# Values, row-tiled sinks and the next scores in one TensorE block, and sink v spread over partitions by DMA

## The chip, the cores and the metric

The kernel runs on one core of a Trainium2 chip. Its time is the device time of one execution in microseconds, and the median of a few executions is given. The core has five engines that work side by side: TensorE (PE) multiplies matrices, VectorE (DVE) and ScalarE (ACT) do elementwise work, GpSimd (POOL) does some too and issues DMAs that change the type, and SyncE (SP) issues DMAs only. Sixteen DMA engines move the data of all queues. TensorE writes to PSUM, which has eight banks of 128 partitions x 512 floats.

## The reference

Attention with a sliding window of 128 positions and 4 sink positions, and then a block of layer norm and MLP, over 4 batches, 8 heads, 768 positions, head size 64:

```python
scores = (1 / sqrt(D)) * q @ k.T                       # per batch and head
keep = (pos_k < 4) | ((pos_q - pos_k >= 0) & (pos_q - pos_k < 128))
a = softmax(where(keep, scores, -1e9))
x = (a @ v), heads side by side                        # (4, 768, 512)
xn = (x - mean(x)) / sqrt(var(x) + 1e-6) * g_ln
out = x + relu(xn @ w_ch1) @ w_ch2                     # w_ch1: 512 x 2048, w_ch2: 2048 x 512
```

## The kernel before

The 768 positions of a batch are 6 tiles of 128, so there are 24 tiles, t = 6 * batch + r. A plan orders all operations: each has a cost, a key (priority) and what it depends on, and the plan lays them out for each engine in the order in which they are then written into the program. The plan's dependencies decide the order only. What an instruction really waits for in the program comes from the buffers that it reads and writes.

The eight PSUM banks are two `wide` buffers of two banks (pool "pw") and four `single` buffers of one (pool "pm").

Scores of a tile: keys of 128 positions against queries of 256, for 8 heads. Two heads stand in the two halves of the 128 partitions, so each matmul has 64 rows:

```python
    def scores(t, halves, key):
        # ... pbs: one wide buffer for each half of the heads; ebs: where exp goes
        def mm(_):
            for pb, eb, part in zip(pbs, ebs, parts):
                # ... (tiles 0 to 2 first add a mask by matmul)
                for i, hp in enumerate([2 * half + i for half in part for i in range(2)]):
                    for h2 in range(2):
                        nc.tensor.matmul(pb.t[:, h2, i],
                                         lhsT=kb.t[64 * h2:64 * (h2 + 1), 1, hp, 128 * r:128 * (r + 1)],
                                         rhs=kb.t[64 * h2:64 * (h2 + 1), 0, hp, 128 * r:128 * r + n],
                                         start=not added, stop=True, skip_group_check=True)
        # ... then ACT takes the exp of each, and DVE or POOL masks it
```

Values of a tile: for each half of the heads (4 heads, 65 columns each: 64 of v and a one, for the sum of the weights), a sink part where r >= 2, the tile's own keys and those of the tile before:

```python
    def values(t, key):
        # ...
        pb = Buf("pw", 0)
        def mm(_):
            # ...
            for half in range(2):
                fresh = True
                if r >= 2:
                    nc.tensor.matmul(po[:, half, 0:4 * (D + 1)], lhsT=esb[b].t[:, 128 * (r - 2):128 * (r - 1)],
                                     rhs=vs[:, 4 * half:4 * half + 4, :].rearrange("p h d -> p (h d)"),
                                     start=True, stop=False, skip_group_check=True)
                    fresh = False
                for hh in range(4):
                    # ... matmul with vn[:, r, h, 0:D + 1], and if r > 0 with vn[:, r - 1, h, 0:D + 1]
        # then on DVE: rc = reciprocal of the sums, xt = values * rc, statistics, xn
```

`esb` holds exp of the sink scores: 8 rows (4 sinks of 2 heads) in each 32 of the 128 partitions. `vs` has the sinks' v at the same rows, each head's in its own rows and zero elsewhere. It is made by a matmul with a 0/1 matrix `sel`, which spreads the 4 sinks' rows of v over the partitions, and a DVE multiply with a mask:

```python
    def sinks(b, key):
        # ...
        def mm_v(_):
            # ...
            for half in range(2):
                nc.tensor.matmul(halves[half][:, 0:4 * (D + 1)], lhsT=sel,
                                 rhs=vn_buf[b % 2][:, 0, 4 * half:4 * half + 4, 0:D + 1],
                                 start=True, stop=True, skip_group_check=True)
        def mul_v(_):
            # ... vs = that * smask, one DVE instruction for each half
        # mm: sink scores, four matmuls of 512 columns into one single bank; ex: their exp
```

In what order a tile's parts come, and the up part of the MLP (the down part is alike):

```python
    def attention(t, key):
        scores(t, (0, 1), key)
        if t % RB:
            values(t - 1, key - 0.5)
        if t % RB == RB - 1:
            values(t, key + 1.0)

    def up(g, h0, key):
        # ... pb = Buf("pm", 0): one single bank
        #     4 matmuls of n columns for each block of 128 hidden units, then relu by ACT or DVE
```

At the start, q and k of the first batch come in pieces over several queues, are cast and transposed by TensorE, while `spin` matmuls of constants keep TensorE busy.

Of the kernel before, what the change touches and what calls it, by code (L numbers as in the profile page):

```python
# [8 lines left out]
FP32 = mybir.dt.float32  # L9
# [22 lines left out]
class Plan:  # L32
# [18 lines left out]
    def op(self, engs, fn, deps=(), key=0.0, alloc=(), uses=(), lat=0.0):  # L51
        o = Op(engs, fn, deps, key, alloc, uses)
        o.lat = lat
        self.ops.append(o)
        return o
# [108 lines left out]
def kernel(  # L164
# [28 lines left out]


    GROUPS = [2, 2, 2, 4, 4, 4, 4, 2]
    NB0 = 3
    NG = len(GROUPS)
    FIRST = [sum(GROUPS[:g]) for g in range(NG)]
# [33 lines left out]
    def room_for(buf):  # L232
        return wide[buf.slot // 2] if buf.pool == "pw" else single[buf.slot - 4]
# [88 lines left out]
    op({"POOL": 0.5}, const_sel, [begun], -499.4)  # L322
    sinks_done = op({"POOL": 0.9}, const_sinks, [begun], -440)

# [89 lines left out]
    def load_w(which, c, key, took=2.6):  # L417
# [7 lines left out]

        w_in[(which, c)] = load(0.85, took, go, key)


    prepped, kqb, turns = {}, {}, {}

# [67 lines left out]
    def sinks(b, key):  # L498

        ks, vs = ks_buf[b % 2], vs_buf[b % 2]  # L500
        kb = kqb[b]
        pb, eb = Buf("pm", 0), Buf("es", 2)
        esb[b] = eb

        def mul_k(_):
            nc.vector.tensor_tensor(
                ks[:, :, 0:2 * NS].rearrange("p a (i s) -> p a i s", i=2),
                kb.t[:, 1, :, 0:NS].unsqueeze(2).to_broadcast([128, HP, 2, NS]),
                hmask.unsqueeze(1).unsqueeze(3).to_broadcast([128, HP, 2, NS]), op=ALU.mult)

        vb = [Buf("pw", 0)] if b else [Buf("pm", 0), Buf("pm", 0)]

        def mm_v(_):
            if b:
                halves = [room_for(vb[0])[:, i] for i in range(2)]
            else:
                halves = [room_for(i) for i in vb]
            vb[0].t = halves
            for half in range(2):
                nc.tensor.matmul(halves[half][:, 0:4 * (D + 1)], lhsT=sel,  # L520
                                 rhs=vn_buf[b % 2][:, 0, 4 * half:4 * half + 4, 0:D + 1],
                                 start=True, stop=True, skip_group_check=True)

        def mul_v(_):
            for half in range(2):
                nc.vector.tensor_tensor(
                    vs[:, 4 * half:4 * half + 4], vb[0].t[half][:, 0:4 * (D + 1)].rearrange("p (h d) -> p h d", d=D + 1),
                    smask[:, 4 * half:4 * half + 4].unsqueeze(2).to_broadcast([128, 4, D + 1]), op=ALU.mult)

        def mm(_):  # L530
            pb.t = room_for(pb)
            for hp in range(HP):
                nc.tensor.matmul(pb.t[32 * hp:32 * (hp + 1), :], lhsT=ks[:, hp, :], rhs=kb.t[:, 0, hp, 256:S],  # L533
                                 start=True, stop=True, skip_group_check=True)

        def ex(_):
            eb.t = espool.tile([128, S - 256], BF16, name="es")
            nc.scalar.activation(eb.t, pb.t, AF.Exp, scale=scale)

        o1 = op({"DVE": 0.2}, mul_k, ready(b, range(HP), 0, NS, 0, 0) + [sunk.get(b - 2), sinks_done, edone.get((RB * b, 0)) if b else None], key, (), [kb])  # L540
        ov = op({"PE": 0.22}, mm_v, [vcast[(b, 0)], sinks_done, ones_done] + ready(b, range(HP), 0, 0, 256, S), key, vb)
        vs_done[b] = op({"DVE": 0.8}, mul_v, [ov, vread.get((b - 2, RB - 1))], key, (), vb)
        o2 = op({"PE": 0.4}, mm, [o1] + ready(b, range(HP), 0, 0, 256, S), key, [pb], [kb])
        sunk[b] = op({"ACT": 0.6}, ex, [o2], key, [eb], [pb])

    ebuf = {}

    def scores(t, halves, key):

        b, r = divmod(t, RB)  # L550
        kb = kqb[b]
# [9 lines left out]
        added = t < NEG_TILES  # L561

        def mm(_):
            for pb, eb, part in zip(pbs, ebs, parts):
                eb.t = epool.tile([128, 2, 512 // n, n], BF16, name="e")
                pb.t = room_for(pb).rearrange("p a (i c) -> p a i c", c=n)
                if added:
                    neg = (neg1 if r else neg0)[:, 0:n].unsqueeze(1).to_broadcast([128, 2, n])
                    for h2 in range(2):
                        nc.tensor.matmul(pb.t[:, h2], lhsT=ident, rhs=neg,  # L570
# [7 lines that stand above are left out]

        cost = 0.2 + 0.23 * n / 256 * len(halves) + (0.43 * len(halves) if added else 0.0)
        hps = [2 * half + i for half in halves for i in range(2)]  # L580
        o0 = op({"PE": cost}, mm, ready(b, hps, 128 * r, 128 * (r + 1), 128 * r, 128 * r + n) + [neg_done, edone.get((t - 1, 1)) if last else None], key, pbs + ebs, [kb])

        for pb, eb, part in zip(pbs, ebs, parts):
            def ex(_, pb=pb, eb=eb):
# [32 lines left out]
    xb, xnb, xtb, mvb, rsb, turned = {}, {}, {}, {}, {}, {}  # L617
    aggr = {}

    def values(t, key):  # L620
        b, r = divmod(t, RB)
        g, ti = where[t]
        vn, vs = vn_buf[b % 2], vs_buf[b % 2]
        pb = Buf("pw", 0)
        xb[t] = Buf("x", 14)
        xnb[t] = Buf("xn", 6)

        def mm(_):
            po = pb.t = room_for(pb)
            pv = po[:, :, 0:4 * (D + 1)].rearrange("p a (h d) -> p a h d", d=D + 1)  # L630
            for half in range(2):
                fresh = True
                if r >= 2:
                    nc.tensor.matmul(po[:, half, 0:4 * (D + 1)], lhsT=esb[b].t[:, 128 * (r - 2):128 * (r - 1)],  # L634
                                     rhs=vs[:, 4 * half:4 * half + 4, :].rearrange("p h d -> p (h d)"),
                                     start=True, stop=False, skip_group_check=True)
                    fresh = False
                for hh in range(4):
                    i, h2 = divmod(hh, 2)
                    h = 4 * half + hh  # L640
                    nc.tensor.matmul(pv[:, half, hh, :], lhsT=weights_of(t, half, i, h2, 0), rhs=vn[:, r, h, 0:D + 1],  # L641
                                     start=fresh and hh == 0, stop=(r == 0), skip_group_check=True)
                    if r > 0:
                        nc.tensor.matmul(pv[:, half, hh, :], lhsT=weights_of(t - 1, half, i, h2, 128),  # L644
                                         rhs=vn[:, r - 1, h, 0:D + 1], start=False, stop=True, skip_group_check=True)

        deps = [edone[(t, half)] for half in range(2)] + [vcast[(b, r)], ones_done]
        uses = [ebuf[(t, half)] for half in range(2)]
# [5 lines left out]
        if r >= 2:  # L654
            deps += [sunk[b], vs_done[b]]
            uses += [esb[b]]
            cost += 0.22
        o = op({"PE": cost}, mm, deps, key, [pb], uses)
        vread[(b, r)] = o

        rc = {}

        def recip(_):
            pv = pb.t[:, :, 0:4 * (D + 1)].rearrange("p a (h d) -> p a h d", d=D + 1)
            rc[0] = small.tile([128, 2, 4], FP32, name="rc")
            nc.vector.reciprocal(rc[0], pv[:, :, :, D])
            xb[t].t = xpool.tile([128, H, D], BF16, name="xt")
            nc.vector.tensor_tensor(xb[t].t.rearrange("p (a h) d -> p a h d", a=2), pv[:, :, :, 0:D],  # L668
                                    rc[0].unsqueeze(3).to_broadcast([128, 2, 4, D]), op=ALU.mult)

# [11 lines left out]
            nc.vector.scalar_tensor_tensor(xnb[t].t, in0=xf, scalar=mvb[g][:, ti, 0:1], in1=gb,  # L682
                                           op0=ALU.subtract, op1=ALU.mult)

        o = op({"DVE": 0.92}, recip, [o], key, [xb[t]], [pb])
        o = op({"DVE": 0.9}, stat, [o], key, (), [xb[t]])
        aggr[t] = o
        o = op({"DVE": 0.75}, cen, [o, gb_done], key, [xnb[t]], [xb[t]])
# [120 lines left out]


    def attention(t, key):
        scores(t, (0, 1), key)
        if t % RB:
            values(t - 1, key - 0.5)
        if t % RB == RB - 1:
            values(t, key + 1.0)


# [22 lines left out]
    for x in range(2):  # L841
        load_runs(1, 0, x, 0, H, 3.85, -436 + x)
    load_w(2, 3, -434)
    for r in range(RB):
        load_v(1, r, -430 + r)

    for b in range(B):
# [25 lines left out]
        if b == 1:  # L873
            for hp in range(HP):
                prep_runs(1, 0, hp, k0 - 12 + 3 * hp)
        else:
            for r in range(RB):
                for x in range(2):
                    load_qk(b, x, r, k0 - 60 + r, [prepped.get((b - 1, RB - 1, 1))])
            for r in range(RB):  # L880
                load_v(b, r, k0 - 50 + r, [prepped[(b, RB - 1, 1)]])
        for r in range(RB):
            attention(RB * b + r, akey(RB * b + r))
            if r == 1:
# [55 lines left out]
```

The softmax here doesn't subtract the row's maximum and nothing guards it: scores larger than these inputs give would overflow.

## Time and profile before

| | |
|---|---|
| time, median of 3 runs | 225.98 us (225.73 to 226.04) |
| span of the profiled execution | 224.5 us |
| TensorE busy | 217.9 us (97%) |
| VectorE, ScalarE, GpSimd busy | 115.3, 111.8, 81.3 us |
| matmuls of the MLP (lines 745 and 785) in the chain that ended last | 34% and 37% |
| bytes moved by DMA | 25.59 MB, 84774 packets |

The profile is of one execution on the chip. A group's line has the source line, engine, operation, the buffers written and read, shapes, count, then busy time and mean duration of one in ns, and the idle time of the engine just before them. A timeline's line has start, duration, engine, source line, operation, buffers and count. Matmuls are pipelined, so their durations overlap: what one costs is read from the start of one to the start of the next.

### The profile page before, as it was taken

The page shows a single profiled execution, that of the slowest core. Times are in us where ns is not written, and L with a number is a line of the kernel's source. Part 1 is how long each engine was busy: PE and PEld are TensorE (multiplying, and loading weights), DVE is VectorE, ACT ScalarE, POOL GpSimd, SP SyncE. Part 2 cuts the span into 40 slices and gives each one's busy share as a digit, 9 for nine tenths or more (in the row PEclk, how much of TensorE's full clock was granted, in tenths as well). Part 3 has the DMA queues.
Part 4 walks back from the last instruction along what each step waited for, and adds up shares of the span by engine and source line. Part 5 has one row for each costly group of instructions (what it writes and reads, how often), then busy time and mean ns, then how long its engine had stood idle before and what let it go on. Part 6 is the DMA issues. An engine that isn't in the chain of part 4 may idle for free.

```text
span 224.5 us, 4431 instructions
## 1 busy us (share of the span) xinstructions
PE 217.9 (97%) x1805; PEld 123.4 (55%) x1826; DVE 115.3 (51%) x216; ACT 111.8 (50%) x159; POOL 81.3 (36%) x111
## 2 busy tenths in 40 slices
PE   8999999999999999999999999999999999999994
PEld 7565878884546455455454444544454554444852
DVE  5556876044978779589574467470026750021011
ACT  3689775677342585870327762147613157400620
POOL 8985976269420699350833000220006020000000
PEclk9999999999999999999999999999999999999999
DMA  6999999999999599999899011230002130012102
GB/s 166 154 190 198 191 206 204 204 160 155 133 137 260 131 151 149 147 131 180 90 170 233 12 23 48 87 103 0 0 36 85 47 96 0 0 47 93 50 0 93
DMA packets 84774, 25.59 MB, mean 114 GB/s; under 512 B 74385, under 2 KB 81809, under 8 KB 84754
## 3 DMA queue, kind: packets, MB, share of 16 engines
q0 software_dynamic: 59392, 13.24, 69.2%
q1 hardware_dynamic: 24818, 11.67, 25.4%
q10 hardware_dynamic: 544, 0.39, 0.5%
q8 instruction: 14, 0.23, 0.4%
q14 instruction: 6, 0.05, 0.1%
HBM read 27.27 MB, written 6.29 MB: 149 GB/s over the span
## 4 chain that ended last, share of the span: by engine, by line
PE 90%; DVE 7%; issue 1%; ACT 0%; DVEq 0%
PE single L785 37%; PE single L745 34%; PE wide L574 5%; PE single L236 3%; PE wide L641 2%; PE wide L644 2%; DVE xn L682 2%; DVE st L674 2%; DVE xt L668 2%; PE wide L634 1%; PE wide L457 1%; PE wide L570 1%; PE single L721 1%; PE single L457 1%; PE single L533 1%
## 5 line engine op out<-in xcount | busy, mean ns | idle before, releaser
L745 PE MATMUL single<-xnt,w1s 128*128 128x256 bf16 (+1 forms) x503 | 87.1, 325 | 0.6 <-issue 0.2
L745 PEld LDWEIGHTS <-w1s 128*128 128x128 bf16 x512 | 48.5, 98 | 32.6 <-issue 1.9
L585 ACT ACTIVATE e<-wide 128x1024 bf16<-128x1024 f32 x44 | 43.7, 1022 | 43.3 <-PE wide L574 40.8
L785 PE MATMUL single<-w2s,h1t 128*128 128x512 bf16 x249 | 57.6, 379 | 0.4
L798 DVE SCALAR_TENSOR_TENSOR ot<-single,rs,xt 128x512 f32<-128x512 f32 (+2 forms) x25 | 18.2, 729 | 60.2 <-PE single L785 45.1
L754 ACT ACTIVATE h1t<-single 128x512 bf16<-128x512 f32 x60 | 35.8, 597 | 20.9 <-PE single L745 20.9
L785 PEld LDWEIGHTS <-h1t 128*128 128x128 bf16 x256 | 24.0, 98 | 28.2 <-issue 1.1
L785 PE MATMUL single<-w2s,h1n 128*128 128x512 bf16 (+2 forms) x139 | 29.6, 355 | 0.3
L754 ACT ACTIVATE h1n<-single 128x512 bf16<-128x512 f32 x30 | 17.9, 597 | 22.2 <-PE single L745 22.0
L597 POOL TENSOR_SCALAR_AFFINE_SELECT e<-e 128x512 bf16<-128x512 bf16 (+1 forms) x10 | 7.1, 713 | 44.8 <-ACT e L585 44.8
L407 POOL DMA_DIRECT2D vn<-in_v_dram x24 | 21.6, 918 | 2.5 <-DMA qkn<-in_q_dram 1.1
L694 POOL TENSOR_SCALAR ve<-mv 128x2 f32<-128x2 f32 (+1 forms) x8 | 4.6, 574 | 45.8 <-DVE mv L677 45.6
L595 DVE TENSOR_TENSOR e<-e,mask 128x1024 bf16<-128x1024 bf16 x22 | 15.9, 722 | 8.7 <-ACT e L585 8.5
L785 PEld LDWEIGHTS <-h1n 128*128 128x128 bf16 x144 | 12.6, 98 | 12.3 <-issue 1.3
L682 DVE SCALAR_TENSOR_TENSOR xn<-xt,mv,gb 128x512 bf16<-128x512 bf16 x24 | 18.6, 780 | 0.8
L674 DVE BATCH_NORM_STATS2 st<-xt 128x6 f32<-128x512 bf16 x24 | 16.7, 695 | 0.8
L668 DVE TENSOR_TENSOR xt<-wide,rc 128x512 bf16<-128x512 f32 x24 | 16.6, 691 | 0.8
L641 PE MATMUL wide<-vn,e 128*128 128x65 bf16 x192 | 15.8, 193 | 0.0
L641 PEld LDWEIGHTS <-e 128*128 128x128 bf16 x192 | 13.7, 97 | 2.6 <-issue 0.2
L574 PE MATMUL wide<-qkt 64*128 64x256 bf16 (+1 forms) x192 | 14.5, 263 | 0.0
L644 PE MATMUL wide<-vn,e 128*128 128x65 bf16 x160 | 14.2, 193 | 0.0
L398 POOL DMA_DIRECT2D qkn<-in_q_dram x12 | 11.3, 940 | 3.5 <-DMA qkn<-in_k_dram 3.0
(66 smaller groups left out, 162.5 us busy)
## 6 DMA issues: line engine op xcount, KB each, us to landing
out_dram<-ot SPq DMA_DIRECT2D x23, 256.0 KB, 2.2
vn<-in_v_dram POOLq DMA_DIRECT2D x24, 128.0 KB, 8.0
w1s<-in_moe_w_ch_dram POOLq DMA_DIRECT2D x4, 512.0 KB, 11.9
w2s<-in_moe_w_ch_dram POOLq DMA_DIRECT2D x4, 512.0 KB, 14.5
qkn<-in_q_dram POOLq DMA_DIRECT2D x12, 128.0 KB, 7.6
qkn<-in_k_dram POOLq DMA_DIRECT2D x12, 128.0 KB, 7.0
qkn<-in_q_dram POOLq DMA_DIRECT2D x1, 768.0 KB, 16.5
qkn<-in_k_dram POOLq DMA_DIRECT2D x1, 768.0 KB, 19.3
```

Of the source, the lines that this page charges most:

```text
L407: nc.gpsimd.dma_start(vn_buf[b % 2][:, r, :, 0:D], v[b, :, 128 * r:128 * (r + 1), :].rearrange("h p d -> p h d"))
L574: nc.tensor.matmul(pb.t[:, h2, i], lhsT=kb.t[64 * h2:64 * (h2 + 1), 1, hp, 128 * r:128 * (r + 1)], rhs=kb.t[64 * h2:64 * (h2 + 1), 0, hp, ...
L585: nc.scalar.activation(eb.t, pb.t, AF.Exp, scale=scale)
L641: nc.tensor.matmul(pv[:, half, hh, :], lhsT=weights_of(t, half, i, h2, 0), rhs=vn[:, r, h, 0:D + 1], start=fresh and hh == 0, stop=(r == 0 ...
L644: nc.tensor.matmul(pv[:, half, hh, :], lhsT=weights_of(t - 1, half, i, h2, 128), rhs=vn[:, r - 1, h, 0:D + 1], start=False, stop=True, ski ...
L668: nc.vector.tensor_tensor(xb[t].t.rearrange("p (a h) d -> p a h d", a=2), pv[:, :, :, 0:D], rc[0].unsqueeze(3).to_broadcast([128, 2, 4, D] ...
L674: nc.vector.bn_stats(st, xf)
L682: nc.vector.scalar_tensor_tensor(xnb[t].t, in0=xf, scalar=mvb[g][:, ti, 0:1], in1=gb, op0=ALU.subtract, op1=ALU.mult)
L745: nc.tensor.matmul(pb.t[:, n * i:n * (i + 1)], lhsT=w1s[:, j, 128 * (h0 + i):128 * (h0 + i + 1)], rhs=xtb[g].t[:, j, 0:n], start=(j == 0), ...
L754: nc.scalar.activation(hb.t, pb.t, AF.Relu)
L785: nc.tensor.matmul(pb.t[:, 0:n], lhsT=hidden(g, ht, ti), rhs=w2s[:, ht, c0:c1], start=(ht == 0), stop=(ht == NH1 - 1))
L798: nc.vector.scalar_tensor_tensor(ob.t[:, 0:n], in0=pb.t[:, 0:n], scalar=rsb[g][:, ti:ti + 1], in1=xb[t].t.rearrange("p h d -> p (h d)")[:, ...
```

## The change

Four things are changed.

- The values of a tile and the scores of the next tile become one block of TensorE instructions, for the values of tiles 10 to 22. The values of tiles 6 to 9 stay alone (`ALONE`), and so does the last tile. The values of the last tile of batches 1 and 2 (tiles 11 and 17) are held back until the scores of the next batch's first tile.
- In a joined block the values are summed in two single banks, not in one wide buffer, and the sinks come last: two matmuls of 64 rows, rows 0 to 63 for heads 0 to 3 and rows 64 to 127 for heads 4 to 7 (the rows of `vs` outside these are zero for these heads). Alone, a sink matmul has 128 rows, as before. They are meant to use TensorE in two row groups, right before the scores, which have 64 rows too.
- For batches 1 to 3, the sinks' v is loaded from DRAM straight into all 128 partitions (four DMAs for a batch, each with 32 copies of one sink's rows, into a buffer of pool "ot"), and one DVE multiply makes `vs` of it. The `sel` matmuls are left out there. The column of ones in the second `vs` buffer is written once at the start.
- The joined values are normalised by DVE in two halves.

```diff
+    ALONE = (6, 7, 8, 9)
...
+    sinks_done = op({"DVE": 0.1}, lambda _: nc.vector.tensor_copy(vs_buf[1][:, :, D], smask), [sinks_done], -90)
...
+    def load_first_v(b, key, deps=()):
+        fb = first_v[b] = Buf("ot", 3)
+        def go(_):
+            fb.t = opool.tile([128, DM], FP32, name="ot")
+            for i in range(NS):
+                src = v[b, :, i, :]
+                nc.sync.dma_start(fb.t.rearrange("(g s) (h d) -> s g h d", s=NS, h=H)[i],
+                                  bass.AP(src.tensor, src.offset, [[0, 128 // NS]] + list(src.ap)))
+        o = op({"SP": 2.0}, go, deps, key, [fb])
+        first_in[b] = op({"XD": 1.0}, None, [o], key, (), [fb], 4.0)
...
+        def pick_v(_):
+            nc.vector.tensor_tensor(vs[:, :, 0:D], first_v[b].t.rearrange("p (h d) -> p h d", h=H),
+                                    smask.unsqueeze(2).to_broadcast([128, H, D]), op=ALU.mult)
...
-        ov = op({"PE": 0.22}, mm_v, ...)
-        vs_done[b] = op({"DVE": 0.8}, mul_v, ...)
+        if b == 0:
+            # ... mm_v and mul_v as before
+        else:
+            vs_done[b] = op({"DVE": 0.6}, pick_v, [first_in[b], sinks_done, vread.get((b - 2, RB - 1))], key, (), [first_v[b]])
...
-    def scores(t, halves, key):
+    def scores(t, halves, key, lead=None):
...
         def mm(_):
+            if lead:
+                lead.fn(None)
...
-    def values(t, key):
+    def values(t, key, joined=False):
...
-        pb = Buf("pw", 0)
+        banks = [Buf("pm", 0), Buf("pm", 0)] if joined else [Buf("pw", 0)]
...
+        def sink(half, fresh):
+            rows = slice(64 * half, 64 * (half + 1)) if joined else slice(0, 128)
+            nc.tensor.matmul(sums[half], lhsT=esb[b].t[rows, 128 * (r - 2):128 * (r - 1)],
+                             rhs=vs[rows, 4 * half:4 * half + 4, :].rearrange("p h d -> p (h d)"),
+                             start=fresh, stop=not fresh, skip_group_check=True)
...
+            if r >= 2 and joined:
+                for half in range(2):
+                    sink(half, False)
...
+            if len(banks) == 2:
+                for half in range(2):
+                    pv = sums[half].rearrange("p (h d) -> p h d", d=D + 1)
+                    rc[half] = small.tile([128, 4], FP32, name=f"rc{half}")
+                    nc.vector.reciprocal(rc[half], pv[:, :, D])
+                    nc.vector.tensor_tensor(xb[t].t[:, 4 * half:4 * half + 4], pv[:, :, 0:D],
+                                            rc[half].unsqueeze(2).to_broadcast([128, 4, D]), op=ALU.mult)
+                return
...
     def attention(t, key):
-        scores(t, (0, 1), key)
-        if t % RB:
+        alone = t - 1 in ALONE
+        scores(t, (0, 1), key, None if alone or t == RB else values(t - 1, key, True))
+        if alone:
             values(t - 1, key - 0.5)
-        if t % RB == RB - 1:
+        if t == NT - 1:
             values(t, key + 1.0)
...
+    load_first_v(1, -424, [w_in[(2, 0)]])
...
             for r in range(RB):
-                load_v(b, r, k0 - 50 + r, [prepped[(b, RB - 1, 1)]])
+                if r == 0:
+                    load_first_v(b, k0 - 43, [vcast[(b - 1, RB - 1)]])
+                load_v(b, r, k0 - 50 + r, [prepped[(b, RB - 1, 1)], turned.get(14)])
```

## The prediction

> **What bounds the kernel now.** I read the page's busy shares and slices first, then the groups of TensorE (matmul) by form, then its timeline in a steady stretch and at the start, and last the SyncE queue and the DMA rates.
>
> ```profile
> PE 217.9 (97%) x1805; PEld 123.4 (55%) x1826; DVE 115.3 (51%) x216; ACT 111.8 (50%) x159; POOL 81.3 (36%) x111
> ...
> PE   8999999999999999999999999999999999999994
> ...
> DMA  6999999999999599999899011230002130012102
> ```
>
> TensorE is busy in every slice but the first and last; no other engine is over 51%. The DMA engines are full up to slice 21 (about 118 us) and mostly idle later. A busy share doesn't say that TensorE does useful work or runs at its peak, so the groups by form come next:
>
> ```profile
> L785 PE MATMUL single<-w2s,h1t 128*128 128x512 bf16 x249 | 57.6, 379 | 0.4
> L745 PE MATMUL single<-xnt,w1s 128*128 128x512 bf16 x247 | 57.1, 379 | 0.6 <-issue 0.2
> ...
> L574 PE MATMUL wide<-qkt 64*128 64x256 bf16 x160 | 12.9, 272 | 0.0
> L634 PE MATMUL wide<-vs,es 128*128 128x260 bf16 x32 | 8.7, 273 | 0.0
> ...
> L520 PE MATMUL wide<-vn,sel 128*128 128x260 bf16 x6 | 1.2, 275 | 0.0
> ```
>
> The MLP's matmuls wait 0.4 and 0.6 us in all. From about 35 us on, TensorE's instructions simply stand back to back, and the end is their sum. The mean ns of a row are latencies and overlap, so I take costs from start to start, as in this stretch of the timeline:
>
> ```profile
> 112.26 0.27 PE L634 MATMUL wide<-vs,es 128*128 128x260 bf16 x1
> 112.37 0.19 PE L641 MATMUL wide<-vn,e 128*128 128x65 bf16 x1
> 112.40 0.19 PE L644 MATMUL wide<-vn,e 128*128 128x65 bf16 x1
> ```
>
> A 260-column sink matmul costs 0.11 us, a 65-column one 0.03. The chain of waits gives the scores block, "121.69 0.54 PE wide L574 x8": eight 256-column matmuls of 64 rows in 0.54 us. A 256-column matmul of 128 rows (L745, "20.53 0.98 PE single L745 x8" or "35.47 3.49 PE single L745 x32") costs 0.109 us, so eight in turn would be 0.87. Two 64-row matmuls do run side by side. From the starts in the trace, going into such a block costs 0.10 us and leaving it 0.10 to 0.15.
>
> Before 20 us TensorE is filled with spinner matmuls (L236), which do nothing but keep it busy: there the bound is loads, casts, exps and DVE. Here is the place that I think decides this case:
>
> ```profile
> 14.54 0.53 PE L457 MATMUL single<-ident,qkn 128*64 128x128 bf16 x12
> ...
> 15.32 0.81 PE L457 MATMUL single<-ident,qkn 128*64 128x128 bf16 x12
> 16.14 0.40 PE L721 MATMUL single<-ident,xn 128*128 128x128 bf16 x4
> ```
>
> The same twelve transposes take 0.53 us once and 0.81 the next time: in the middle of the second group TensorE waits for a k load of batch 0, which lands at 15.73. The transposes of xn follow with no gap. So that load has no slack. And the SyncE queue at the start:
>
> ```profile
> 0.80 0.97 SPq L376 DMA_DIRECT2D ot<-in_k_dram  x2
> 1.81 0.36 SPq L829 DMA_DIRECT2D grow<-in_moe_g_ln_dram  x1
> 53.65 5.73 SPq L481 DMA_TRANSPOSE qkt<-qkn  x4
> ```
>
> Between 2.2 and 53.6 us SyncE issues nothing at all. The DMA engines meanwhile, by stages (the last two columns are their busy share and GB/s):
>
> ```profile
> core 0: us, PE busy (x) PEld busy (x) DVE busy (x) ACT busy (x) POOL busy (x), PEclk, DMA share, GB/s
> 4.00:6.00 2.00, 2.00 (x28) 1.64 (x27) 1.27 (x3) 1.02 (x2) 2.00 (x4) 1.00 1.27 215
> 6.00:8.00 2.00, 2.00 (x24) 1.04 (x21) 0.82 (x2) 0.96 (x2) 2.00 (x3) 1.00 1.37 147
> 8.00:10.00 2.00, 2.00 (x33) 1.14 (x33) 1.06 (x3) 0.96 (x2) 2.00 (x4) 1.00 1.65 162
> ```
>
> A share over 1 means that an engine has more than one packet under way. They are full from the start.
>
> **What the Trainium skill says.** "TensorE: Matmul & The Clock Gate", Part 3 (Packing small matmuls): matmuls in different row groups run concurrently, some 4 ns apart. The trace agrees (0.54 against 0.87 us above). "TensorEngine Tiling (Array Packing)", Key Properties: a change of the tiling mode drains TensorE; the trace has 0.10 us at the entry. The same page, Gotcha 1: row tiles must write different PSUM banks, which is why the joined sum takes two single banks. "DMA: Bandwidth & Descriptors", Queues, rings and completion order (Arbitration): each DMA engine takes turns between the queues that have work. The trace has no early SyncE traffic beside a full GpSimd queue after 5 us, so it can't confirm this; in this case it matters most.
>
> **The change part by part.** I laid the two built programs' TensorE instructions side by side.
>
> 1. *Sink v no longer through TensorE (batches 1 to 3).* Six 260-column matmuls (L520 x6) leave: 6 x 0.111 = 0.67 us saved. In their place stand four DMAs (each writes the eight heads' rows of one sink to 32 partitions) and one DVE multiply of 512 columns for each batch in place of two of 260. DVE is at 51% and its part isn't on the path.
>
> 2. *Row-tiled sinks.* Thirteen value blocks are joined to the next tile's scores; nine of them have sinks. Each has two 260-column matmuls of 128 rows, which become two of 64 rows in different row groups: 0.11 in place of 0.22 us, so 9 x 0.11 = 1.00 us saved. The other seven pairs stay as they are.
>
> 3. *The order.* Values of 128 rows, then sinks and scores of 64: one entry and one exit, as before, so joining saves no mode change of itself. It only keeps the row-tiled sinks from costing one of their own. In batch 2 the sink scores (L533) now stand directly after a scores block: one switch less, 0.10 us.
>
> 4. *DVE.* A joined sum is normalised in two halves of four instructions, not two: estimated from the 0.21 us of the reciprocal and 0.69 us of the multiply at 13.42 and 13.66 in DVE's timeline at about 1.2 us in place of 0.9, 13 x 0.3 = 4 us more of DVE, which has 109 us free. No effect, unless a bank comes free too late for the next up or down block. A held-back last v (tiles 11 and 17) comes 7 us later, but its group's MLP is over 20 us away. The order shows no place where I find less than about 0.3 us of room; I allow 0.1 us for small stalls.
>
> Sum on TensorE: 0.67 + 1.00 + 0.10 = 1.77 us saved, of which all is on the path, since that path is TensorE's sum.
>
> 5. *The spread loads.* The plan gives them a late place (after the w2 load), but that is an order in the plan, not a wait. In the built program they stand in SyncE's queue right behind the load of g, for batch 1 **and** batch 2, eight DMAs of 64 KB. The first three wait for nothing, the others only for the first q and k loads and one DVE cast, all over by 5.4 us. So 512 KB in 2048 pieces of 256 bytes goes out between about 2.2 and 7 us, into DMA engines that the GpSimd queue already fills. Size of it: in the trace's packet records a 768-byte packet of the SyncE queue took 36 ns, a 256-byte one 18 ns; 2048 / 16 engines = 128 packets an engine if they are spread evenly, x 18 ns = 2.3 us. By bytes: between 5 and 6.5 us the GpSimd queue took 35 ns for a piece that reads 768 bytes, 22 GB/s an engine, and 32 KB an engine at that rate is 1.5 us. I take 1.9. DMA engines that are full stay full, so the k load of 15.73 lands about 1.9 us later, and with it the transposes, ScalarE's copies and exps (packed from 15 to 24 us) and the start of the dense MLP at 20.5. Nothing later can take it back: from 35 us TensorE has no idle time. Added: 1.9 us.
>
> Sum: 225.98 - 1.77 + 0.10 + 1.90 = 226.2; I lean a little to the side of the loads hiding in part, and say **226.0**.
>
> **The rivals.**
>
> *(A) The loads hide.* The early engines may have room: at 7.0 to 7.5 us the queue moved little over half its usual packets, and batch 0's earlier loads have about 0.8 us to spare. Against it: the shares of 1.27 to 1.65 above, and no slack at 15.73. If it holds, only the saving is left: 224.2 to 224.5.
>
> *(B) The loads cost more than their size.* Each 256-byte run is read 32 times from the same place, and small packets alternate with the critical ones. A wait in the start that lets TensorE idle could also bring its clock down, which now reads 9 in all slices. For it speaks only that the start is the one place without slack: 227 to 228.
>
> *(C) Row tiles don't overlap* because both sinks' weights are loaded just before. Against it: the scores do just that with eight loads in 0.54 us. It would take back 1.0 us: 227.
>
> *(D) Two of four single banks taken by values stall the MLP.* Its matmuls need a bank every 0.87 us and a relu takes 0.6; DVE holds the two for 0.8 and 1.4 us. The other two are enough for a scores block (0.75 us with its switches) and one up block. At 0.1 to 0.3 us in a few of 13 blocks: up to 1 us more.
>
> **Range and chances.** Saving 1.77, give or take 0.3; delay 0 to 3, most of it between 1.2 and 2.3; stalls 0 to 1. Four fifths: 224.3 to 227.6 us. Two per cent is 4.5 us: below 221.5 there is no sum that leads there, and above 230.5 only a stall that I can't see. Faster 0.02, same 0.95, slower 0.03.
>
> **What would show it.** Right in steps 1 and 2: no sel matmuls for batches 1 to 3; two row-tiled sinks 64 rows high whose starts are a few ns apart, and 0.11 us to the first score. Right in step 5: SyncE's queue busy with the spread loads at 2 to 7 us, the k load of 15.73 landing at 17 or later, the first up block (L745, at 20.46) late by the same, and the stretch from there to the end shorter by 1.7. Wrong: an unchanged time of the first up block (then A, and the time is under 224.6), a shortening of the dense stretch under 1 us (C or D), or idle time of TensorE ended by DVE or ACT after 50 us.

## The result and the profile after

The changed kernel takes 234.0 us (median of 4 runs, 233.4 to 234.5), the kernel before 226.0 us on the same chip (4 runs, 225.7 to 226.6). The ratio is 1.035, 95% interval 1.032 to 1.038: 8.0 us slower, where the prediction had 226.0 us and a range up to 227.6.

From the page of the kernel after, the busy shares and the slices:

```profile
PE 218.3 (94%) x1798; PEld 124.0 (53%) x1820; DVE 115.3 (50%) x236; ACT 112.3 (48%) x159; POOL 87.2 (37%) x118
...
PE   8969999999999999999909999999999999999994
...
PEclk9999999999999999999985999999999999999999
```

TensorE is busy for as long as before (218.3 against 217.9 us), and its share falls only because the span grew. The rows of slices, counted from 0, say where: in slice 20 (116 to 122 us) TensorE is idle and the mean granted clock is down to 8 tenths, and in slice 21 it is 5. Before, TensorE was busy in these slices and the clock row was full. The page's group of the up matmuls names what ended the idle time; the kernel before comes first, then the one after:

```profile
PEclk9999999999999999999999999999999999999999
...
L745 PE MATMUL single<-xnt,w1s 128*128 128x256 bf16 (+1 forms) x503 | 87.1, 325 | 0.6 <-issue 0.2
```

```profile
L808 PE MATMUL single<-xnt,w1s 128*128 128x256 bf16 (+1 forms) x504 | 88.9, 331 | 6.0 <-DMA xnt<-xn 5.4
```

6.0 us of idle time ahead of these matmuls, against 0.6 before, 5.4 of it ended by a DMA that writes `xnt`: the transposed, normalised tiles that the up part reads. TensorE's timeline there:

```profile
114.39 0.28 PE L665 MATMUL single<-vs,es 64*128 64x260 bf16 x2
114.51 0.39 PE L598 MATMUL wide<-qkt 64*128 64x128 bf16 x8
114.83 1.90 PE L848 MATMUL single<-w2s,h1t 128*128 128x512 bf16 x8
122.11 0.58 PE L808 MATMUL single<-xnt,w1s 128*128 128x512 bf16 x1 [5.38 <-DMA xnt<-xn]
122.91 1.49 PE L808 MATMUL single<-xnt,w1s 128*128 128x512 bf16 x3 [0.22 <-issue]
```

The first two lines are the new block at work: two row-tiled sinks, and 0.12 us after the first of them the first score, as foreseen. Then comes a single wait of 5.4 us of idle time (5.5 us if it is counted from the start of one matmul to the start of the next, less what the matmul itself takes; waits outside the views are counted so below). It is the first up block of group 4 (tiles 10 to 13), which needs tile 13. And after it three matmuls take 1.49 us where eight took 1.90: from 122.1 to 127.6 us the matmuls of 512 columns start every 0.43 us and not every 0.22. The granted clock is half from 120.9 to 127.7 us.

Why is tile 13 late? Its `xn` was ready at 99.58 us (99.22 before), in good time. SyncE's queue of the kernel before, and then of the one after:

```profile
87.59 18.51 SPq L481 DMA_TRANSPOSE qkt<-qkn  x12
106.20 4.42 SPq L711 DMA_TRANSPOSE xnt<-xn  x3
```

```profile
93.44 19.70 SPq L500 DMA_TRANSPOSE qkt<-qkn  x12
113.23 1.22 SPq L774 DMA_TRANSPOSE xnt<-xn  x1
...
115.13 2.99 SPq L774 DMA_TRANSPOSE xnt<-xn  x2
```

In both kernels tile 13's transpose stands behind the twelve q/k transposes of batch 3, each of which needs a load of q or k to have landed. Before, it was issued at 109.38 and landed at 114.19, and TensorE wanted it at 115.4, when the last matmul ahead of the block started: about 1.2 us of slack. After, it is issued at 115.13 (the first of the two in the last line) and lands at 121.86, and TensorE wants it, by the same measure, at 116.35. So it is issued 5.75 us later, and it also takes 6.7 us to land instead of 4.8.

The q/k transposes are late because batch 3's q and k loads are. Those are issued by GpSimd, whose queue shows what they stand behind; first before, then after:

```profile
75.10 1.04 POOL L696 TENSOR_TENSOR rs<-ve,neg_half 128x4 f32<-128x4 f32 x1
76.12 5.36 POOL L407 DMA_DIRECT2D vn<-in_v_dram  x6
81.41 0.94 POOL L398 DMA_DIRECT2D qkn<-in_q_dram  x1
```

```profile
78.42 1.04 POOL L759 TENSOR_TENSOR rs<-ve,neg_half 128x4 f32<-128x4 f32 x1
79.44 1.08 POOL L626 TENSOR_SCALAR_AFFINE_SELECT e<-e 128x1024 bf16<-128x1024 bf16 x1
80.48 5.36 POOL L410 DMA_DIRECT2D vn<-in_v_dram  x6
85.77 0.95 POOL L401 DMA_DIRECT2D qkn<-in_q_dram  x1
```

Batch 2's v loads go out 4.4 us later, and the two lines ahead of them say why. The plan now puts the mask of tile 11's exps (L626) ahead of the loads; it takes 1.0 us. The other 3.3 us are the delay of `rs`, which needs DVE's statistics of tile 9, and so its values on TensorE. In the changed program the values of tile 9 stand behind the scores of tile 10 and no longer ahead of them. Their first sink, before and after:

```profile
70.24 0.27 PE L634 MATMUL wide<-vs,es 128*128 128x260 bf16 x1
```

```profile
74.66 0.27 PE L665 MATMUL wide<-vs,es 128*128 128x260 bf16 x1
```

Of these 4.4 us, 1.9 are the late start. With the v loads batch 3's q and k loads slip from 81.41 to 85.77; the last of these lands at 110.72, not 104.90. The four spread loads of batch 3 go out through SyncE meanwhile (87.4 to 90.0 us).

At the start, TensorE and the SyncE queue look like this (two views of the kernel after):

```profile
14.32 0.42 PE L682 MATMUL wide<-vn,e 128*128 128x65 bf16 x8 [1.39 <-DMA vn<-in_v_dram]
...
16.01 0.20 PE L682 MATMUL wide<-vn,e 128*128 128x65 bf16 x1 [0.60 <-DMA vn<-in_v_dram]
```

```profile
2.22 5.64 SPq L441 DMA_DIRECT2D ot<-in_v_dram  x8
```

The spread loads stand at 2.2 to 7.9 us and TensorE waits 1.99 us for v loads of batch 0: the first landed at 12.15 before and lands at 14.27 now, the second went from 12.99 to 15.97. The k load at 15.73 moved to 17.79. The first up block starts at 22.38 instead of 20.46. What the spread loads bring isn't used until DVE makes `vs` of it, at 41.7 us for batch 1 and 62.8 us for batch 2.

The books, in us against the kernel before:

| term | predicted | measured | from |
|---|---|---|---|
| `sel` matmuls gone | -0.67 | -0.68 | starts of the six matmuls before |
| one switch less in batch 2 | -0.10 | -0.10 | scores block to up block before, 88.7 to 89.2; after, the sink scores follow the scores directly |
| row-tiled sinks | -1.00 | -0.90 | starts of all 32 sinks: 3.54 before, 2.64 after |
| start | +1.90 | +1.92 | first up block |
| wait of group 4 | 0.1 for all stalls | +5.5 | starts, 116.35 to 122.11, less the matmul between |
| slow clock after it | none | +2.8 | run `spins` below |
| sum | +0.2 | +8.5 | measured in the runs: +8.0; in the profiled executions +8.3 |

### The profile page after: what moved, and what is told of

Read it like the earlier page. It is cut to its first block, busy times and chain, and to the rows that moved or that the text cites. A ratio compares the mean times of both kernels' runs of the same rounds, so it can differ in the third digit from the quotient of the medians.

```text
span 232.8 us, 4480 instructions
## 1 busy us (share of the span) xinstructions
PE 218.3 (94%) x1798; PEld 124.0 (53%) x1820; DVE 115.3 (50%) x236; ACT 112.3 (48%) x159; POOL 87.2 (37%) x118
## 4 chain that ended last, share of the span: by engine, by line
PE 80%; DMA 7%; DVE 5%; POOL 3%; issue 2%; ACT 1%; SPq 0%; DVEq 0%
PE single L848 35%; PE single L808 33%; DMA qkn<-in_k_dram 4%; PE wide L598 4%; DMA xnt<-xn 3%; POOL qkn L361 2%; PE single L682 1%; DVE xn L745 1%; DVE st L737 1%; PE single L685 1%; PE wide L476 1%; ACT qkt L223 1%; DVE xt L731 1%; PE single L665 1%; PE single L784 1%
## 5 line engine op out<-in xcount | busy, mean ns | idle before, releaser
L808 PE MATMUL single<-xnt,w1s 128*128 128x256 bf16 (+1 forms) x504 | 88.9, 331 | 6.0 <-DMA xnt<-xn 5.4
L808 PEld LDWEIGHTS <-w1s 128*128 128x128 bf16 x512 | 49.5, 99 | 41.7 <-issue 11.2
L848 PE MATMUL single<-w2s,h1t 128*128 128x512 bf16 x248 | 56.0, 379 | 0.8 <-issue 0.6
L626 POOL TENSOR_SCALAR_AFFINE_SELECT e<-e 128x512 bf16<-128x512 bf16 (+1 forms) x14 | 10.1, 724 | 46.3 <-ACT e L614 46.2
L745 DVE SCALAR_TENSOR_TENSOR xn<-xt,mv,gb 128x512 bf16<-128x512 bf16 x24 | 20.0, 833 | 0.9 <-DVE mv L740 0.3
L724 DVE RECIPROCAL rc<-single 128x4 f32<-128x4 f32 x26 | 4.6, 176 | 23.3 <-PE single L665 16.9
L682 PEld LDWEIGHTS <-e 128*128 128x128 bf16 x192 | 13.1, 98 | 4.8 <-DMA vn<-in_v_dram 2.3
L624 DVE TENSOR_TENSOR e<-e,mask 128x1024 bf16<-128x1024 bf16 x18 | 12.4, 689 | 5.8 <-ACT e L614 5.7
L401 POOL DMA_DIRECT2D qkn<-in_k_dram x12 | 11.1, 922 | 2.2 <-DMA w2s<-in_moe_w_ch_dram 1.7
L685 PEld LDWEIGHTS <-e 128*128 128x128 bf16 x160 | 10.7, 97 | 1.6
```

The lines of the kernel that those rows point to most:

```text
L401: nc.gpsimd.dma_start(dst[:, r], (q, k)[x][b, :, 128 * r:128 * (r + 1), :].rearrange("h p d -> p h d"))
L682: nc.tensor.matmul(pv[:, hh, :], lhsT=weights_of(t, half, i, h2, 0), rhs=vn[:, r, h, 0:D + 1], start=fresh and hh == 0, stop=(r == 0), ski ...
L685: nc.tensor.matmul(pv[:, hh, :], lhsT=weights_of(t - 1, half, i, h2, 128), rhs=vn[:, r - 1, h, 0:D + 1], start=False, stop=not (joined and ...
L808: nc.tensor.matmul(pb.t[:, n * i:n * (i + 1)], lhsT=w1s[:, j, 128 * (h0 + i):128 * (h0 + i + 1)], rhs=xtb[g].t[:, j, 0:n], start=(j == 0), ...
L848: nc.tensor.matmul(pb.t[:, 0:n], lhsT=hidden(g, ht, ti), rhs=w2s[:, ht, c0:c1], start=(ht == 0), stop=(ht == NH1 - 1))
```

## The experiments

Three theories. **Theory 1**: tile 13's transpose comes late through the chain of queues above, and the wait brings the clock down; joined blocks as such are innocent. **Theory 2**: the joined blocks, their single banks and DVE's extra work are to blame. **Theory 3**: the late start alone sets off everything. Runs of one group shared a chip and its runs of the kernel before (226.1, 226.1 and 226.3 us).

### One half at a time

`no_spread` keeps the joined blocks and takes the spread loads out:

```diff
-        if b == 0:
+        if True:                     # mm_v with sel and mul_v in every batch
...
-    load_first_v(1, -424, [w_in[(2, 0)]])
...
-                if r == 0:
-                    load_first_v(b, k0 - 43, [vcast[(b - 1, RB - 1)]])
```

> The joined blocks stay, the spread loads go (sink v by the sel matmuls again, in all batches). Theory 1 (the loss is the wait of group 4's first up block for tile 13's transposed xn, 5.4 us, the slow clock after it, some 3 us, and 1.9 us at the start; the late transposes come from a pile-up in SyncE's and GpSimd's queues): the 1.9 us at the start are gone, 0.67 us of sel matmuls are back, and as only a part of the pile-up is gone, the wait shrinks to 0 to 3 us: 225.5 to 230. Theory 2 (the joined blocks in single banks are to blame themselves): 231 or more. Theory 3 (the delay at the start alone sets off everything later): no wait at all, 225.0.

Measured: 228.79 us, ratio 1.011 (1.008 to 1.013), in the range of theory 1. Tile 13 lands at 117.86, and group 4 waits 1.7 us; the clock stays at 9. Later 1.0 us more goes to a bank that comes late. Without spread loads the wait is shorter but not gone: v loads of batch 2 go out at 78.26, also behind the mask, and tile 9's values (72.38) stand behind tile 10's scores here too.

`not_joined` keeps the spread loads and undoes the joining:

```diff
-        alone = t - 1 in ALONE
-        scores(t, (0, 1), key, None if alone or t == RB else values(t - 1, key, True))
-        if alone:
+        scores(t, (0, 1), key)
+        if t % RB:
             values(t - 1, key - 0.5)
-        if t == NT - 1:
+        if t % RB == RB - 1:
             values(t, key + 1.0)
```

> The spread loads stay, the joined blocks go (values alone in a wide bank with sinks of 128 rows, at the places of the kernel before). Theory 1: 1.9 us lost at the start, 0.67 won, the wait of group 4 for its transposes gone or under 2 us: 227 to 229.5. Theory 2: 227.2. Theory 3: the wait stays, 233 or more.

Measured: 235.1 us, ratio 1.036 (1.029 to 1.044), as slow as the whole change. No joined block is left, and yet group 4 waits 4.1 us for tile 13 (landing at 121.59, v loads at 80.65). The clock reads 7 in one slice at the start and in one after this wait. Theory 2 falls as the cause of the wait. The time is the one that theory 3 gave; theory 1 had wrongly expected the wait to shrink without the joining, so this run alone doesn't decide between the two.

`late_spread` keeps everything, but holds the spread loads of batches 1 and 2 until 50 us and later:

```diff
+        def hold(_):
             fb.t = opool.tile([128, DM], FP32, name="ot")
+            nc.vector.memset(fb.t[:, 0:1], 0.0)
+        def go(_):
...
-    load_first_v(1, -424, [w_in[(2, 0)]])
...
+            load_first_v(1, k0 - 1, [prepped[(1, 0, HP - 1, 1)]])
...
-                    load_first_v(b, k0 - 43, [vcast[(b - 1, RB - 1)]])
+                    load_first_v(b, k0 - 43, [vcast[(b - 1, RB - 1)], vs_done[b - 1]])
```

> The changed kernel, with the spread loads of batches 1 and 2 held back by a small DVE memset of their buffer, so that they go out after 50 us. Theory 1: the first up block is back at 20.5 us (1.9 us won), the wait of group 4 stays about as it is: 231.5 to 232.5. Theory 2: the same. Theory 3: without the delay at the start the wait is gone as well: 224.2.

Measured: 241.0 us, ratio 1.063 (1.057 to 1.069), slower still and outside all three expectations. The first up block is back at 21.15, but a new wait appears at about 70 us, probably because a spread load now takes one of the three `ot` buffers in a stretch in which DVE needs them for outputs (this was not tested): DVE waits 4.2 us for `out_dram<-ot` and TensorE 3.4 us for DVE's `xn` at 69 us. Group 4 waits 6.5 us. A wait, moved, is not a wait removed. Theory 3 can't be judged from it alone, since the edit made a wait of its own.

### Cures

`early_turn` puts tile 13's transposes (and so tile 12's) ahead of the second half of batch 3's q/k transposes in SyncE's order, nothing else:

```diff
-        o = op({"SP": 1.25}, go, [lo], key, alloc, [kb, qb])
+        o = op({"SP": 1.25}, go, [lo] + ([turning[13]] if b == 3 and r >= 3 else []), key, alloc, [kb, qb])
...
+            turning[t] = o           # the op of xn's transpose of tile t
```

> The changed kernel, with the DMA transposes of tiles 12 and 13 put ahead of batch 3's q and k transposes of rows 3 to 5 in SyncE's queue; nothing else is meant to change. Theory 1: the wait of 5.4 us and the slow clock behind it go, the 1.9 us at the start stay: 225.5 to 226.5. Theories 2 and 3: the order of these transposes matters little, 231 or more.

Measured: 226.73 us, ratio 1.001 (0.999 to 1.004): 7.3 of the 8.0 us are back by the order of two small DMAs. SyncE's queue:

```profile
93.33 9.60 SPq L500 DMA_TRANSPOSE qkt<-qkn  x6
103.06 2.70 SPq L774 DMA_TRANSPOSE xnt<-xn  x2
106.28 5.68 SPq L500 DMA_TRANSPOSE qkt<-qkn  x4
```

Tile 13's transpose now goes out at 104.4. The loads are as late as ever (v of batch 2 at 80.44), the start too (22.41), and the clock reads 9 throughout. What remains over the prediction's sum, 226.2, is mostly a wait of 0.85 us for a bank at 118.9.

`v2_early` leaves SyncE's order alone and frees the other end of the chain, the place of batch 2's v loads in GpSimd's queue; `nospread_v2` does the same without spread loads:

```diff
-                load_v(b, r, k0 - 50 + r, [prepped[(b, RB - 1, 1)], turned.get(14)])
+                load_v(b, r, k0 - 50 + r, [prepped[(b, RB - 1, 1)] if b > 2 else None, turned.get(14)])
```

> The changed kernel, spread loads and joined blocks kept, SyncE's order of transposes untouched; only batch 2's v loads no longer have to stand behind batch 2's last transposes in the plan, so that they, and batch 3's q and k loads behind them in GpSimd's queue, are issued earlier. If the chain is as I read it (late v loads of batch 2 on GpSimd, then batch 3's loads, then its transposes on SyncE, then tile 13's), the wait of group 4 goes though nothing at SyncE was reordered: 225.7 to 226.5 us, as early_turn. If the order at SyncE alone is what matters, it stays near 234.

> Joined blocks kept, no spread loads (as in no_spread, 228.79 us, where group 4 waits 1.7 us), and batch 2's v loads in the plan no longer behind batch 2's last transposes, so that GpSimd issues them at about 60 us and batch 3's q and k loads at some 78 to 90 us. If the wait of group 4 comes down GpSimd's queue, it goes: 225 to 226 us. If the earlier v loads crowd batch 2's own loads and the output stores, as in v2_early (234.84), it is slower than no_spread.

Measured: 234.84 us (1.032 to 1.043) and 228.47 us (1.007 to 1.014), both slower than the 225 to 226.5 us that the chain by itself would give. Group 4's wait is gone in both, but only the second shows why: there v loads go out at 57.5 and tile 13 lands at 108.06, well before TensorE needs it. In `v2_early` TensorE itself came to group 4 some 8 us later, mostly because of a new wait of 4.8 us at 74 us, so it proves nothing about the chain. The expectation of `v2_early` had no place for the new wait. As the queues read, v loads crowd batch 2's own loads, SyncE's transposes wait for those, the output stores stand behind the transposes, and DVE has no output buffer. In DVE's timeline of `v2_early`:

```profile
75.79 0.75 DVE L861 SCALAR_TENSOR_TENSOR ot<-single,rs,xt 128x512 f32<-128x512 f32 x1 [5.74 <-DMA out_dram<-ot]
```

`nospread_v2` pays 1.3 us for the same at 73.6 us and is no faster than `no_spread`.

### Each suspect in the kernel before

`before_loads` is the kernel before with the eight spread loads added and nothing else:

```diff
+    load_first_v(1, -424, [w_in[(2, 0)]])
+    load_first_v(2, -423, [w_in[(2, 0)]])
     for r in range(RB):
         load_v(1, r, -430 + r)
```

> The kernel before with nothing but the eight spread loads of batches 1 and 2 added behind the load of g in SyncE's queue; nobody reads them, every other engine's order is as before. Step 5 of the prediction alone. The k load of 15.73 us lands, and the first up block starts, some 1.9 us later. Theory 1: TensorE and the loads of the later batches move together, tile 13's slack of about 1.2 us stays, no wait of group 4: 226.0 + 1.9 = 227.9 us. Theory 3 (the late start alone sets off the wait): 233 us or more. Rival A (loads hide): 226.

Measured: 229.45 us, ratio 1.016 (1.011 to 1.020). TensorE waits for a v load of batch 0, and the clock reads 8 in two slices there:

```profile
15.09 0.62 PE L656 MATMUL wide<-vn,e 128*128 128x65 bf16 x8 [2.33 <-DMA vn<-in_v_dram]
...
PEclk9988999999999999999999999999999999999999
```

After that wait of 2.3 us the first up block starts at 23.45, 3.0 us late. From there to the last matmul it takes 200.85 us, before 200.77: nothing else follows. So the start costs more here than in the changed kernel, 3 us and not 1.9, but it sets off no wait of group 4: tile 13 and TensorE slip together. Theory 3 falls.

`before_late_v` is the kernel before, with batch 2's v loads put behind the mask of tile 11's exps in GpSimd's order:

```diff
-                load_v(b, r, k0 - 50 + r, [prepped[(b, RB - 1, 1)]])
+                load_v(b, r, k0 - 50 + r, [prepped[(b, RB - 1, 1)]] + ([edone[(RB * b - 1, half)] for half in range(2)] if b == 2 else []))
```

> The kernel before, but in GpSimd's order batch 2's v loads stand behind the mask of tile 11's exps, as they do in the changed kernel; no other load and no joined block. If that place in the queue makes the wait (theory 1), batch 2's v loads go out some 4 us later (80 instead of 76 us), batch 3's q and k loads and their transposes too, and tile 13 is turned at 117 to 119 us where TensorE wants it at 115.5: a wait of 2 to 4 us in a kernel that has none of the change's parts, and with it 228.5 to 231 us (more if the clock falls). If the late v loads are harmless, 226.

Measured: 235.2 us, ratio 1.039 (1.036 to 1.043). More than expected: the v loads went out at 84.17, not 80, since tile 11's scores come at 81.5 us here, as before, and its mask only then; in the changed kernel they come at 76.9. The waits of TensorE:

```profile
PE single L533 <- DMA qkt<-qkn: 4.1, 1, 4.1
PE single L745 <- DMA xnt<-xn: 1.4, 1, 1.4
```

First batch 3's last q/k transposes are missing, then tile 13 (issued 118.62, landing 124.45), and the clock reads 7 and 5 afterwards. So late v loads alone, with no other part of the change, bring on the waits and the slow clock, and cost 9 us. They don't size the mask's part in the change: here the v loads go out 8.1 us later than in the kernel before, in the changed kernel 4.4, and most of the wait here is for q and k.

### The size of two terms, and both cures together

`spins` fills group 4's wait with matmuls of constants:

```diff
+            if g == 4 and h0 == 0:
+                for _ in range(90):
+                    nc.tensor.matmul(pb.t[:, 0:128], lhsT=spinner, rhs=spinner, start=True, stop=True, skip_group_check=True)
```

> The changed kernel with 90 matmuls of constants (128 columns, some 5 us) put ahead of the first up block of group 4, where TensorE otherwise waits 5.4 us for the transposed tile 13. Work, loads and buffers are otherwise the same. If the wait costs its own length alone, the time stays at 234 us. If the idle time also brings TensorE's clock down afterwards (theory 1: 8 and 5 tenths in two slices, some 2.9 us), the clock should stay at 9 and the time fall to about 231 us. If the matmuls come to more than the wait, the excess is added: up to 0.5 us.

Measured: 232.4 us, ratio 1.028 (1.023 to 1.032). TensorE's timeline:

```profile
117.67 5.19 PE L808 MATMUL single<-spinner 128*128 128x128 bf16 x90
122.87 3.40 PE L811 MATMUL single<-xnt,w1s 128*128 128x512 bf16 x15
```

Fifteen up matmuls in 3.40 us, full speed, and the clock reads 9 everywhere. This run had a wait of 1.3 us of its own at 99 us, so the sound comparison is from group 4's first up block to the last matmul: 104.9 us here, 107.7 in the changed kernel. The slow clock costs 2.8 us. The Trainium skill ("TensorE: Matmul & The Clock Gate", Part 1) says that the clock halves after an idle window of some 3.4 us and comes back after such a window of sustained work. The trace agrees with the halving (0.43 against 0.22 us a matmul). On the length of the wait the runs differ from the page: every wait of 3.4 us or more was followed by slices under 9, and one of 1.7 us in the dense stretch (`no_spread`) was not, but at the start a wait of 2.3 us was followed by two slices of 8 (`before_loads`) and one of 1.45 us by a slice of 7 (`v2_early`). The two waits of 1.39 and 0.60 us in the changed kernel's start left the clock at 9. So these runs give no threshold. The slow stretch of 5.5 us was longer than one such window.

`turn_full` is `early_turn` with sinks of 128 rows in the joined blocks:

```diff
-            rows = slice(64 * half, 64 * (half + 1)) if joined else slice(0, 128)
+            rows = slice(0, 128)
```

> As early_turn (the transposes of tiles 12 and 13 ahead of batch 3's last q/k transposes in SyncE's order), but the sinks of the joined blocks have 128 rows again, as alone. It sizes the term of the row-tiled sinks: nine pairs, each two matmuls one after the other (0.22 us) instead of side by side (0.11 us), so 9 x 0.11 = 1.0 us more than early_turn's 226.73, about 227.7 us. If row tiles gain nothing here (rival C of the prediction): 226.7. Above 228.5 something else would have moved with it.

Measured: 227.81 us, ratio 1.007 (1.005 to 1.009), 1.1 us over `early_turn`. The traces give 0.9 us for the sinks themselves: from the last value matmul to the first score it takes 0.35 us here and 0.25 in `early_turn`, in nine blocks. The row tiles are worth about what was predicted.

`nospread_turn` has the edits of `no_spread` and `early_turn` together:

```diff
-        if b == 0:
+        if True:
...
-    load_first_v(1, -424, [w_in[(2, 0)]])
...
+        o = op({"SP": 1.25}, go, [lo] + ([turning[13]] if b == 3 and r >= 3 else []), key, alloc, [kb, qb])
```

> Joined blocks and row-tiled sinks kept, sink v through TensorE in all batches (no spread loads), and the transposes of tiles 12 and 13 early as in early_turn. Theory 1: both costs are gone, the 1.9 us at the start and the wait of group 4; left are the savings of steps 2 and 3 (1.1 us) less small stalls (up to 0.8 us, as at 118.9 us in early_turn): 224.9 to 225.8 us, a little under the kernel before. If the spread loads' place at the start costs nothing by itself (rival A), it would be early_turn's 226.7 plus 0.67 for the matmuls, about 227.4.

Measured: 225.77 us, ratio 0.998 (0.997 to 1.000): 0.3 us under the kernel before, with an interval that just reaches it. The first up block is at 20.52. Of the 1.1 us that steps 2 and 3 save, 0.6 goes to two small waits for DVE and POOL (0.33 at 77.2 and 0.29 at 87.1). `early_turn`, which has the spread loads, takes 1.0 us more: they cost more at the start (1.9 us) than the 0.67 us of matmuls that they replace.

## Why the prediction was wrong

1. *`sel` matmuls* and 2. *row-tiled sinks*: right in mechanism and size. The stated sign, a first score 0.11 us after the first sink, came at 0.12, and `turn_full` confirms the size (0.9 us in the traces, 1.1 between the medians). The two single banks don't follow from the row tiles, though: the two halves of a wide buffer already lie in two banks.
3. *Order*: right. In batch 2 the sink scores follow a scores block directly, at 88.25 us.
4. *DVE, room*: here the prediction failed. Its words were "The order shows no place where I find less than about 0.3 us of room; I allow 0.1 us for small stalls". I looked for room at the banks, at DVE and on TensorE, and for a held-back v I asked how far away its group's MLP was. I never asked how much time lay between the landing of a tile's transpose and its use, though the trace had it: tile 13, 1.2 us. In place of 0.1 us for stalls, the runs showed a wait of 5.5 us there and 2.8 us of slow clock behind it. The sign of being wrong that the prediction named for late stalls, idle time ended by DVE or ACT, left out DMAs, and a DMA ended this one. DVE's work on tile 13 was harmless (its `xn` was ready only 0.4 us later). Its work on tile 9 was not: the program had moved that tile's values, and with them `rs`, which holds up GpSimd's queue.
5. *Spread loads*: right in size in the changed kernel (1.92 us), wrong in the load that carries it: TensorE waits for v of batch 0, ahead of the k load that I named. Rival A gave the earlier loads about 0.8 us to spare; they slipped by 2.1 and 3.0. Alone in the kernel before the spread loads cost 3 us, so the agreement is partly luck: in the seven traces with early spread loads the first up block starts at 22.1 to 23.5 us, in the six others at 20.5 to 21.2. "Nothing later can take it back" holds; the error was to think that nothing later would be added.

Rival B had one part of it, a wait that brings the clock down, but placed at the start, where it came about in `before_loads` and not in the changed kernel. None of the rivals named a change of order in GpSimd's queue, although the two programs could be laid side by side for GpSimd as they were for TensorE: the mask of tile 11 stands ahead of the v loads there. And the DMA engines' full slices up to 118 us, which the prediction quotes, suggest that loads up to there have little room to catch up: in the changed kernel the first q load of batch 3 was issued 4.4 us later, and the last k load landed 5.8 us later.

The last link is shown by `early_turn`, which took away the wait and 7.3 us by moving two transposes. The links ahead of it are shown in direction (`before_late_v`, `nospread_v2`), not in size. What stays open: both `no_spread` and `not_joined` have the mask ahead of the v loads and tile 9's values late, while the eight spread loads alone (`before_loads`) leave GpSimd's order as it was. So either half of the change moves these, or something that both runs kept does; which cost or key in the plan it is wasn't tried.

## What to carry to other kernels

Before judging that a change is off the path, list for every DMA that feeds the bound engine its landing and the moment of use, and carry the change through each issuing queue, not through the compute engines alone. A queue that issues in order hands every delay to whatever stands behind: tile 13 was ready at 99.6 us and went out at 115.1. And price a long wait on TensorE with the slow clock after it: 5.5 us of waiting cost 8.3 here.

## What the runs showed of the hardware

- After the wait of 5.4 us TensorE ran at half speed for 5.5 us (0.43 us per 512-column matmul); with matmuls of constants in the gap it didn't.
- 512 KB in 256-byte pieces from SyncE delayed v loads of the full GpSimd queue by 2.1 and 3.0 us in one trace, and TensorE's start by 1.9 to 3.0 us. The Trainium skill ("DMA: Bandwidth & Descriptors", Queues, rings and completion order) has the engines take turns between queues; this agrees, where the kernel before could not say.
